# Row stores of tiles 20 to 27 moved from the last attention group to behind the last group's logits

## Chip, cores and metric

The kernel runs on one core of one Trainium2 chip. The metric is the device time of one execution in microseconds (us); the median of several runs is compared.

## The reference

Block-local attention is followed by a mixture of experts that sends each token to one expert. Cut to what matters:

```python
def _attn_ref(q, k, v):              # 8 batches, 8 heads, 576 tokens, 64 dims, chunks of 64
    scores = scale * np.matmul(q_c, k_c.transpose(0, 1, 2, 4, 3))
    attn = softmax(scores)           # over the 64 keys of a chunk
    return np.matmul(attn, v_c)

def _moe_ref(x, w_gate, w1, w2):     # x: 4608 x 512, 8 experts, hidden 1024
    logits = x @ w_gate
    expert_idx = np.argmax(logits, axis=1)
    gate_w = softmax(logits)[arange, expert_idx]
    for e in range(E):
        xe = x[expert_idx == e]
        out[expert_idx == e] = gate_w * (np.maximum(xe @ w1[e], 0) @ w2[e])
```

## The kernel before

**Two phases.** The attention makes 36 tiles of 128 token rows, two tiles (one group) at a time, in the loop `for g in range(NG)` (L1033, 18 groups) and in the straight code behind it (L1098 to L1155), which finishes groups 16 and 17. The experts' phase takes the rows back in expert order, one slot of 256 rows (and up to 128 more) after another. Slot 0 (expert 0) runs already in the gaps of the last groups: `filler(n)` issues n halves of its matmul blocks (L622 and L720 to L722). Slot 1 begins after `make_xt(1, ...)`, L1171 to L1173.

**A group's way.** scores (L238), softmax, transpose (L274), attention times V (`attn_v`, L286), the sums on ScalarE (`soft_d`, L264 and L265), reciprocal (L266) and products (`x_out`, L298 and L301) on VectorE, which write the tile into a row buffer `xb`. Then `x_t` (L310) transposes the tile, `logits` (L322, copied at L1007) computes the gate, `sel_` (L991) and `sums` (L998) collect it.

**Routing.** The tiles are gathered into batches of 6, 6, 6, 6, 4, 4, 2 and 2. When a batch's last logits are summed, the generator `route` is started; `small_op(n)` issues n of its VectorE steps, `advance` its ScalarE and TensorE steps. It ends with `di`, the row of each token in the expert-sorted scratch `xd` in DRAM (L402); `di` has three buffers, so batch 6 writes the one that batch 3 used, and batch 7 that of batch 4. Then GpSimd copies the gate weight and row number into the tile (L404) and the batch's tiles are appended to the list `waiting`.

**Row stores.** `store(n)` (L419) issues an indirect DMA from GpSimd for each of the first n tiles in `waiting` (L426): 128 rows of 528 floats to their places in `xd`. In the loop there is one call at the top of each group (L1038): 2 tiles, in the last group 4. Before it GpSimd makes a one-element copy (`relay`, L1037) that waits for an earlier group's logits copy. Behind the loop there is a call `store(NMAX)` (NMAX is 6) after each of the logits of group 16 (L1114) and 17 (L1127), one at L1139 and one in each turn of the while loop (L1151). Counting through the generators, `waiting` holds tiles 20 to 23 at the top of the last group, 24 to 27 at L1114, 28 to 31 at L1127, 32 and 33 at L1139, and 34 and 35 in the while loop.

**What comes behind the stores.** Every engine works through its instructions in the order in which they are issued here. `gather(1)` (L1153, DMA at L547) brings the rows of slot 1 from `xd`. It may read any row, so it waits until all 36 stores have landed. After it come `gather_x(1)` and the weight loads `load_w(2, 0)` and `load_w(2, 1)` (L529), and on TensorE the transposes of the gathered rows (L570, L605). VectorE computes `early(1)` and `tables` (L482 to L932) as side work once batch 7 is routed; slot 1 needs their results.

Of the kernel before, what the change touches and what calls it, by code (L numbers as in the profile page):

```python
# [25 lines left out]
NG = NTILE // G  # L26
# [4 lines left out]
NMAX = max(BATCHES)  # L31
# [15 lines left out]
def attn_moe_kernel(ctx: ExitStack, tc: tile.TileContext, q, k, v, wg, w, out):  # L47
# [151 lines left out]
    def load_qk(g):  # L199
        if g:  # L200
            qt[g] = ep.tile([P, G, 512], F32, name="qt", bufs=NK)

        if g >= NK:
            nc.sync.dma_start(kb[g % NK], k[g])
            nc.sync.dma_start(qt[g], q[g])
            return
        for i in range(G):
            nc.sync.dma_start(kb[g % NK][:, i, :], k[g, :, i, :])
            if g:
                nc.sync.dma_start(qt[g][:, i, :], q[g, :, i, :])  # L210

    def load_v(g):
        for m in range(2):
            nc.sync.dma_start(vb[g % NB][m::2, m, :, :], v[g, m::2, :, :])
# [10 lines left out]
    def keep(n):  # L225

        for _ in range(n):
            nc.tensor.matmul(pR.rearrange("p (a b) -> p a b", b=P), ones,
                             ones.unsqueeze(1).broadcast_to([P, 4, P]), start=True, stop=True)

    def scores(g):
        ps = pair
        if g == 3:
            nc.tensor.addr_align(64, offset=48, max_nops=0)
        for i in range(G):
            for hp in range(4):
                for po, m, fo, pi, fi, at_ in quads(i, hp):
                    nc.tensor.matmul(ps[po, m, fo], qt[g][pi, i, fi], kb[g % NK][pi, i, fi],  # L238
                                     start=True, stop=True, tile_position=at_)
        return ps  # L240
# [7 lines left out]
    def soft_a(ps):  # L248
        mx = sm.tile([P, NH, 1], F32, name="mx", bufs=2)
        ex = sp.tile([P, NH // 2, 64, 2], F32, name="ex", bufs=2)  # L250
        p4 = ps.rearrange("p m (h k) -> p m h k", k=64)
        m4 = mx.rearrange("p (m h) o -> p m h o", m=2)
        nc.vector.tensor_reduce(m4.rearrange("p m h o -> p m (h o)"), p4, AX.X, ALU.max)
        nc.vector.tensor_tensor(ex.rearrange("p h k m -> p m h k"), p4, m4.broadcast_to(p4.shape), ALU.subtract)
        return ex

    def soft_b(ex):
        nc.scalar.activation(ex, ex, AF.Exp, scale=0.125)
# [10 lines left out]
    def attn_t(ex, banks="UV"):  # L269
        at = sp.tile([P, G, 4, 128], F32, name="at", bufs=1)  # L270
        for i in range(G):
            pt = bank(banks[i], [P, 4, 128])
            for hp in range(4):
                nc.tensor.transpose(pt[:, hp, :], ex[:, i * 4 + hp, :, :].rearrange("p k m -> p (k m)"), ident)  # L274
            nc.scalar.copy(at[:, i, :, :], pt)
        return at
# [3 lines left out]
    def attn_v(g, at):  # L280
        for i in range(G):
            for hp in range(4):
                to = one["UV"[i]][:, hp * 130:(hp + 1) * 130] if hp < 3 else px3[:, i * 131:i * 131 + 130]
                for c in range(2):
                    po = slice(c * 64, (c + 1) * 64)
                    nc.tensor.matmul(to[po, :], at[:, i, hp, po], vb[g % NB][:, :, hp * 2 + c, i * 65:i * 65 + 65],  # L286
                                     start=True, stop=True, tile_position=(0, c * 64))
# [17 lines left out]
    def x_t(g, xt):  # L305
        xT = sp.tile([P, 4, G * P], F32, name="xT1", bufs=1)
        for i in range(G):
            pxt = bank("TQ", [P, 4, 128])
            for kc in range(4):
                nc.tensor.transpose(pxt[:, kc, :], xt[:, (g * G + i) % RB, kc * 128:(kc + 1) * 128],  # L310
                                    ident)
            nc.scalar.copy(xT[:, :, i * P:(i + 1) * P], pxt)
        return xT
# [105 lines left out]
    def store(n, after=None):  # L419

        for k, (b, i, t, di) in enumerate(waiting[:n]):
            x = xb[t // RB % XB][:, t % RB, :]
            if k == 0 and after is not None:
                nc.scalar.copy(x[:, XW - 1:XW], after)
            stored.add(t)
            nc.gpsimd.indirect_dma_start(  # L426
                out=xds[t],
                out_offset=bass.IndirectOffsetOnAxis(ap=di[:, i, :], axis=0),
                in_=x, in_offset=None, bounds_check=NT - 1, oob_is_err=False)
        del waiting[:n]  # L430
# [4 lines left out]
    def advance(kind, side=False):  # L435


        for x in active:
            if x[1] == kind and x[2] == side and not (kind == "t" and r_live[0]):
                x[1] = next(x[0], "end")  # L440
                if x[1] == "end":
                    active.remove(x)
                return
# [3 lines left out]
    def small_op(n=1):  # L447

        for _ in range(min(n, pace[0])):
            advance("v")  # L450
            pace[0] -= 1
# [536 lines left out]
    def sel_(g):  # L988
        lp = st_l.pop(g)
        for i in range(G):  # L990
            nc.tensor.transpose(p4[:, 3 * i, :], lp[:, i * P:(i + 1) * P], ident)  # L991

    def sums(g):
        b = [i for i in range(NBAT) if first[i] <= g * G][-1]
        if g * G == first[b]:
            lgs[0] = sm.tile([P, NMAX, E], F32, name="lg", bufs=2)[:, 0:BATCHES[b], :]
        o = g * G - first[b]
        nc.vector.tensor_reduce(lgs[0][:, o:o + G, :],  # L998
                                p4.rearrange("p a (c e) -> p a e c", e=32)[:, 0::3, 0:E, :], AX.X, ALU.add)
        if (g + 1) * G == first[b + 1]:  # L1000
            r = route(b, lgs[0])
            active.append([r, next(r), False])

    def logits(g):
        if g in st_x:
            lp, pp = logits_p(g, st_x.pop(g))
            nc.scalar.copy(lp, pp)  # L1007
            st_l[g] = lp

    def pauses():  # L1010
        for x in list(active):
            if x[1] is None:
                x[1] = next(x[0], "end")
                if x[1] == "end":
                    active.remove(x)
# [17 lines left out]
    for g in range(NG):  # L1033
        ga, gl = g - 1, g - 2
        pace[0] = 1000
        if waiting:
            nc.gpsimd.tensor_copy(relay, st_l[gl - 1][:, 0:1])  # L1037
        store(2 if g + 1 < NG else 4)  # L1038
        ps = scores(g)
        keep((6, 0, 0)[min(g, 2)])  # L1040
        if g + NK < NG:
            load_qk(g + NK)
        if g + 1 < NG:
            load_v(g + 1)
        if g == 0:
            nc.sync.dma_start(wg_sb[:, :, 0:E], wg)
        if g == 2:
            nc.gpsimd.memset(oh_b, 0.0)
            for t in (*xg[0], *xg[1], xg3):
                nc.gpsimd.memset(t, 0.0)  # L1050

        if gl >= 1:
            sel_(gl - 1)
        if ga >= 0:
            at = attn_t(st_e[ga])
            if g + 1 == NG:
                st_e[g] = soft_a(ps)
            st_e.pop(ga)
        if gl >= 0:
            st_x[gl] = x_t(gl, xb[gl * G // RB % XB])  # L1060
        if g + 1 < NG:
            st_e[g] = soft_a(ps)
            soft_b(st_e[g])
        else:
            soft_b(st_e[g])

            c2.close()
            psum = ctx.enter_context(tc.tile_pool(name="psum", bufs=1, space=PSUM))
            slots["S"] = [psum.tile([P, 512], F32, name=f"psS{i}") for i in range(2)]
            turns["S"] = 0  # L1070
        if gl >= 1:
            sums(gl - 1)
        pauses()
        for x in casts:
            next(x, None)
        casts.clear()
        advance("t")
        if g + 1 < NG:
            small_op(5)
        if ga >= 0:  # L1080
            attn_v(ga, at)
            ri = soft_d()
        if g + 1 == NG:

            c3.close()
            xtp = ctx.enter_context(tc.tile_pool(name="xtp", bufs=1, side="right", reuse_waits="tile"))
            hp_ = ctx.enter_context(tc.tile_pool(name="hp", bufs=HB, side="right", reuse_waits="tile"))
            xhi = xtp.tile([P, 4, BLK + EXT], F32R, name="xhi")
            xlo = xtp.tile([P, 4, BLK + EXT], F32R, name="xlo")
        logits(gl)  # L1090
        cast(g)
        if ga >= 0:
            x_out(ga, ri, xb[ga * G // RB % XB])
        small_op(2)
        advance("a")
        side_op(4)

    g = NG - 1  # L1098
# [12 lines left out]
    logits(g - 1)  # L1111
    x_out(g, ri, xb[g * G // RB % XB])
    small_op(5)
    store(NMAX)  # L1114
    filler(2)
    sel_(g - 1)
    sums(g - 1)
# [195 lines left out]
```

## Time and profile before

| what | us |
|---|---|
| median of 3 runs | 574.8 |
| the runs | 572.28, 574.8, 576.16 |
| profiled execution, its own time | 572.48 |
| its span, first to last instruction | 570.2 |
| TensorE busy in the span | 552.2 |
| VectorE busy | 405.9 |
| ScalarE busy | 281.9 |
| GpSimd busy | 239.2 |

Times in the trace count from the start of the span. PE is TensorE, PEld its weight loads, DVE VectorE, ACT ScalarE, POOL GpSimd. In a timeline a row gives start, duration, engine, line, operation, output<-inputs, the count of merged instructions, and in brackets how long the engine had been idle and whose event came last before it went on ("issue": nothing that the profile shows). An indirect DMA's row on POOL is the time to issue it, not that of its transfer.

### The profile page before, as it was taken

How to read it: one execution, taken by the hardware profiler on the slowest of the kernel's cores; microseconds unless marked ns; L12 is line 12 of the kernel's file. 1: busy time of each engine (PE TensorE's matmuls, PEld its weight loads, DVE VectorE, ACT ScalarE, POOL GpSimd, SP SyncE). 2: the span in 40 equal slices, each digit the busy share in tenths (PEclk: the TensorE clock that was granted, in tenths of full speed). 3: DMA queues.
4: the chain of work that ended last, by engine and by line, in shares of the span. 5: the costliest groups of instructions: out<-in, count | busy, mean ns of one | idle time of the engine just before them, and what ended most of it. 6: DMA issues, size and time to landing. Idle time of an engine off the chain costs nothing.

```text
span 570.2 us, 13170 instructions
## 1 busy us (share of the span) xinstructions
PE 552.2 (97%) x4699; PEld 488.0 (86%) x4699; DVE 405.9 (71%) x907; ACT 281.9 (49%) x519; POOL 239.2 (42%) x271
## 2 busy tenths in 40 slices
PE   7999999869999999999999999999999999999995
PEld 5888888758798899899998999898999988898994
DVE  6788889634776987888867875676757566766663
ACT  5587877522134644646544654354434344444332
POOL 3036753745424553354440843162425235251422
PEclk9999999979999999999999999999999999999998
DMA  8999999333575632236534543465622346211201
GB/s 308 395 366 368 410 408 396 112 123 125 197 252 185 219 99 61 76 115 207 164 94 165 208 123 123 131 236 182 225 58 81 115 152 217 63 42 29 67 1 58
DMA packets 46564, 99.17 MB, mean 174 GB/s; under 512 B 13184, under 2 KB 26496, under 8 KB 42880
## 3 DMA queue, kind: packets, MB, share of 16 engines
q0 software_dynamic: 18352, 58.30, 29.2%
q1 hardware_dynamic: 27824, 38.98, 19.5%
q8 instruction: 67, 1.10, 0.8%
q10 hardware_dynamic: 288, 0.52, 0.2%
q14 instruction: 33, 0.27, 0.1%
HBM read 106.73 MB, written 20.22 MB: 223 GB/s over the span
## 4 chain that ended last, share of the span: by engine, by line
PE 85%; issue 6%; DVE 3%; DMA 2%; POOL 1%; ACT 1%; another core or an unknown queue 0%; POOLq 0%; DVEq 0%; SPq 0%; ACTq 0%
PE psS L622 24%; PE psL L622 8%; PE psU L722 4%; PE psU L720 4%; PE psU L721 4%; PE psV L720 4%; PE psV L721 4%; PE psV L722 4%; PE psS L238 3%; PE psU L286 2%; PE psV L286 2%; PE psL L322 2%; PE psK L735 2%; PE psK L733 2%; PE psS L626 2%
## 5 line engine op out<-in xcount | busy, mean ns | idle before, releaser
L77 DVE TENSOR_TENSOR wlo<-raw,whi 128x1024 fp32r<-128x1024 f32 x110 | 134.3, 1221 | 17.0 <-ACT whi L76 12.2
L671 ACT ACTIVATE h<-psS 128x384 fp32r<-128x384 f32 x84 | 41.3, 492 | 172.5 <-issue 127.6
L529 POOL DMA_INDIRECT raw<-in_w,widx x58 | 66.4, 1145 | 121.3 <-DVE wlo L77 54.1
L622 PE MATMUL psS<-xhi,whi 128*128 128x256 f32 (+2 forms) x368 | 114.4, 313 | 1.4 <-issue 0.7
L76 ACT CAST whi<-raw 128x1024 fp32r<-128x1024 f32 x110 | 114.8, 1043 | 0.3 <-issue 0.3
L622 PE MATMUL psS<-xhi,wlo 128*128 128x256 f32 (+2 forms) x368 | 113.6, 311 | 0.7 <-issue 0.7
L622 PE MATMUL psS<-xlo,whi 128*128 128x256 f32 (+2 forms) x312 | 96.8, 310 | 0.4 <-issue 0.4
L748 POOL DMA_INDIRECT out_y<-y,oid x40 | 42.4, 1060 | 107.0 <-ACTq L653 34.5
L630 DVE SCALAR_TENSOR_TENSOR hl<-psS,h 128x256 fp32r<-128x256 f32 x84 | 35.6, 424 | 59.1 <-ACT h L671 57.2
L547 POOL DMA_INDIRECT xg<-xd,idx x49 | 63.4, 1295 | 30.7 <-issue 16.7
L622 PEld LDWEIGHTS psS<-xhi,whi 128*128 128x128 f32 x368 | 69.9, 190 | 5.4 <-DVE h L630 0.8
L622 PEld LDWEIGHTS psS<-xhi,wlo 128*128 128x128 f32 x368 | 69.7, 189 | 1.5 <-issue 0.9
L622 PEld LDWEIGHTS psS<-xlo,whi 128*128 128x128 f32 x312 | 59.1, 189 | 3.6 <-issue 1.2
L720 PE MATMUL psU<-whi,h 128*128 128x512 f32 x120 | 48.4, 403 | 0.0
L720 PE MATMUL psV<-whi,h 128*128 128x512 f32 x120 | 47.3, 395 | 0.0
L721 PE MATMUL psU<-wlo,h 128*128 128x512 f32 x120 | 47.3, 394 | 0.0
L721 PE MATMUL psV<-wlo,h 128*128 128x512 f32 x120 | 47.1, 393 | 0.0
L722 PE MATMUL psU<-whi,hl 128*128 128x512 f32 x112 | 44.1, 393 | 0.0
L722 PE MATMUL psV<-whi,hl 128*128 128x512 f32 x112 | 44.0, 393 | 0.0
L426 POOL DMA_INDIRECT xd<-xb,di x32 | 31.6, 987 | 16.1 <-issue 12.9
L622 PE MATMUL psL<-xhi,whi 128*128 128x320 f32 (+2 forms) x112 | 34.9, 312 | 0.0
L622 PE MATMUL psL<-xlo,whi 128*128 128x320 f32 (+2 forms) x112 | 34.9, 312 | 0.0
(253 smaller groups left out, 1111.6 us busy)
## 6 DMA issues: line engine op xcount, KB each, us to landing
vb<-in_v SPq DMA_DIRECT2D x36, 260.0 KB
kb<-in_k SPq DMA_DIRECT2D x16, 512.0 KB
qt<-in_q SPq DMA_DIRECT2D x16, 512.0 KB
xg<-xg SPq DMA_DIRECT2D x208, 32.0 KB
raw<-in_w SPq DMA_DIRECT2D x16, 256.0 KB
kb<-in_k SPq DMA_DIRECT2D x4, 256.0 KB
raw<-in_w,widx POOLq DMA_INDIRECT x58
xg<-xd,idx POOLq DMA_INDIRECT x49
```

The costliest lines, as they stand in the source:

```text
L76: nc.scalar.copy(hi, src)
L77: nc.vector.tensor_tensor(lo, src, hi.bitcast(F32), ALU.subtract)
L426: nc.gpsimd.indirect_dma_start(out=xds[t], out_offset=bass.IndirectOffsetOnAxis(ap=di[:, i, :], axis=0), in_=x, in_offset=None, bounds_che ...
L529: nc.gpsimd.indirect_dma_start(out=raw[c][:, :], out_offset=None, in_=w, in_offset=bass.IndirectOffsetOnAxis(ap=widx[:, u, c:c + 1], axis= ...
L547: nc.gpsimd.indirect_dma_start(out=t[:, :], out_offset=None, in_=xd[0:rows, :], in_offset=bass.IndirectOffsetOnAxis(ap=place(u, h), axis=0 ...
L622: nc.tensor.matmul(ph, a, b[:, kc, WIDE - ph.shape[1]:WIDE], start=kc + i == 0, stop=kc + i == 5 and not late)
L630: nc.vector.scalar_tensor_tensor(o, ph, 0.0, hi.bitcast(F32), ALU.max, ALU.subtract)
L671: nc.scalar.activation(hx[:, EXT:EXT + WIDE], ph, AF.Relu)
L720: nc.tensor.matmul(py, hh, wh, start=f == 0, stop=False)
L721: nc.tensor.matmul(py, hh, wl, start=False, stop=False)
L722: nc.tensor.matmul(py, hl, wh, start=False, stop=f == 7)
L748: nc.gpsimd.indirect_dma_start(out=outs[m], out_offset=bass.IndirectOffsetOnAxis(ap=oid[u % 3][:, m:m + 1], axis=0), in_=y, in_offset=None ...
```

## The change

The call at the top of the last group stores nothing (the tiles stay in `waiting`), and the call after group 16's logits is gone. Tiles 20 to 27 thus stay in the list until the call at L1127, which takes six tiles at a time.

```diff
         if waiting:
             nc.gpsimd.tensor_copy(relay, st_l[gl - 1][:, 0:1])
-        store(2 if g + 1 < NG else 4)
+        store(2 if g + 1 < NG else 0)
         ps = scores(g)
@@
     logits(g - 1)
     x_out(g, ri, xb[g * G // RB % XB])
     small_op(5)
-    store(NMAX)
     filler(2)
     sel_(g - 1)
```

By the list's order the calls now take: L1127 tiles 20 to 25, L1139 tiles 26 to 31, the first turn of the while loop 32 and 33, a later turn 34 and 35. The number of stores, their sizes and their order are as before.

## Rows read from the trace of the kernel before

**Rows 1.** The page: the span, and the chain that ended last, by engine

```profile
span 570.2 us, 13170 instructions
PE 85%; issue 6%; DVE 3%; DMA 2%; POOL 1%; ACT 1%; another core or an unknown queue 0%; POOLq 0%; DVEq 0%; SPq 0%; ACTq 0%
```

**Rows 2.** Busy time by stretch, of the last group and what follows it

```profile
core 0: us, PE busy (x) PEld busy (x) DVE busy (x) ACT busy (x) POOL busy (x), PEclk, DMA share, GB/s
115.00:122.00 7.00, 4.15 (x30) 2.31 (x26) 0.08 (x2) 0.18 (x1) 5.21 (x9) 0.97 0.55 211
122.00:128.00 6.00, 4.13 (x18) 3.74 (x19) 4.06 (x19) 2.31 (x9) 0.31 (x2) 0.50 0.06 23
132.00:140.00 8.00, 7.60 (x52) 6.22 (x50) 2.80 (x19) 1.05 (x8) 5.40 (x9) 1.00 0.54 206
140.00:150.00 10.00, 10.00 (x62) 8.95 (x63) 8.93 (x51) 1.49 (x4) 5.36 (x6) 1.00 0.34 107
```

**Rows 3.** Timeline of POOL: stores, the copy for batch 5, first gather of slot 1

```profile
110.83 1.02 POOL L426 DMA_INDIRECT xd<-xb,di  x1 [0.16 <-issue]
...
118.84 0.98 POOL L426 DMA_INDIRECT xd<-xb,di  x1 [0.30 <-issue]
120.12 0.97 POOL L426 DMA_INDIRECT xd<-xb,di  x1 [0.30 <-issue]
...
127.46 0.31 POOL L404 COPY xb<-ft 128x4 f32<-128x4 f32 x2 [6.17 <-DVE ft L393]
131.03 0.99 POOL L426 DMA_INDIRECT xd<-xb,di  x1 [3.26 <-issue]
...
137.73 0.97 POOL L426 DMA_INDIRECT xd<-xb,di  x1 [0.30 <-issue]
...
141.96 0.97 POOL L426 DMA_INDIRECT xd<-xb,di  x1 [0.30 <-issue]
145.68 1.03 POOL L547 DMA_INDIRECT xg<-xd,idx  x1 [2.75 <-DVE ns L869]
```

**Rows 4.** Timeline of all engines beside the first eight stores

```profile
112.77 0.89 PE L286 MATMUL psU<-vb,at 128*64 128x130 f32 x12
...
115.10 0.39 PE L286 MATMUL psT<-vb,at 128*64 128x130 f32 x4
...
118.09 0.18 ACT L264 ACTIVATE su<-psU 128x6 f32<-128x6 f32 x1 [3.49 <-PE psL L322]
...
119.48 0.38 PE L622 MATMUL psS<-xhi,wlo 128*128 128x256 f32 x1 [0.69 <-issue]
...
122.46 0.17 ACT L265 ACTIVATE su<-psT 128x2 f32<-128x2 f32 x1 [4.19 <-PE psS L622]
...
122.80 0.25 DVE L266 RECIPROCAL ri<-su 128x16 f32<-128x16 f32 x1 [7.72 <-ACT su L265]
```

**Rows 5.** Timeline of an earlier group, with a pair of stores

```profile
86.73 0.98 POOL L426 DMA_INDIRECT xd<-xb,di  x1 [0.31 <-issue]
...
88.82 0.39 PE L286 MATMUL psT<-vb,at 128*64 128x130 f32 x4
...
89.67 0.16 ACT L264 ACTIVATE su<-psU 128x6 f32<-128x6 f32 x1
...
90.04 0.25 DVE L266 RECIPROCAL ri<-su 128x16 f32<-128x16 f32 x1
```

**Rows 6.** Timeline from group 17's logits to slot 1's transposes

```profile
128.75 0.64 PE L322 MATMUL psL<-xT,wg_sb 128*32 128x256 f32 x8
...
134.17 0.17 DVE L402 TENSOR_REDUCE di<-dst 128x2 int32<-128x16 f32 x1 [0.50 <-DMA xd<-xb,di]
...
139.00 0.39 ACT L633 ACTIVATE h<-psS 128x256 fp32r<-128x256 f32 x1 [5.05 <-PE psS L622]
...
139.76 0.16 DVE L402 TENSOR_REDUCE di<-dst 128x2 int32<-128x16 f32 x1
...
149.88 0.63 PE L570 MATMUL psQ<-ident,xg 128*128 128x128 f32 x4
...
150.53 0.14 DVE L932 CAST kind<-vb 128x1 int32<-128x1 f32 x1
```

**Rows 7.** Chain in order of time (start, duration, what): a store's landing

```profile
131.03 2.59 DMA xd<-xb,di
```

## The prediction

> **What bounds the kernel now.** I read the page first: the chain that ended last is TensorE for 85% of a span of 570.2 us [rows 1]. So a change pays by the time at which TensorE gets on with the experts' slots, and the place where this change can move that is the stretch from the last group to slot 1's transposes, about 110 to 156 us. From slot 1 on nothing is edited, and I carry any gain or loss at slot 1's start to the end one for one.
>
> The table by stretch shows what is wrong there [rows 2]. From 115 to 122 us TensorE is busy only 4.15 of 7 us, VectorE 0.08 and ScalarE 0.18, while GpSimd is busy 5.21. Right behind it, from 122 to 128 us, TensorE's granted clock is 0.50. From 132 us on TensorE is full again (7.60 of 8, 10.00 of 10): it has slot 0's fillers.
>
> The timeline of that hole [rows 4]: TensorE's products for psU start at 112.77 and for psT end at 115.10 + 0.39 = 115.49, yet ScalarE reads psU only at 118.09 and psT at 122.46, and VectorE's reciprocal, idle for 7.72 us, comes at 122.80. TensorE itself stops 0.69 us for "issue" before matmuls whose operands are long there. In an earlier group the same ScalarE read comes at 89.67, 0.46 us behind the end of psT (88.82 + 0.39 = 89.21), and the reciprocal at 90.04, 0.83 behind it; a pair of stores had just been issued there too, the second at 86.73 [rows 5]. What is particular to the last group is a train of eight stores, the first at 110.83 and the last at 120.12, with two more just ahead of it [rows 3]. A second train (six stores, 131.03 to 137.73, with a shorter wait at 5.05 us on ScalarE until 139.00 [rows 3, 6]) also makes results come late, but TensorE runs on. So I take the trains as the cause: results of TensorE come late while more than a pair of stores is under way. The trace shows this as a coincidence in time, twice; it shows no mechanism.
>
> **What the change removes.** The train at 110.83 goes. If it is the cause, the reciprocal comes 0.83 us behind psT as in the earlier group, at 115.49 + 0.83 = 116.3 instead of 122.80: 6.5 us earlier. TensorE then doesn't go hungry, and the stretch at half clock goes too: 4.13 us of busy time at 0.50 [rows 2] would be about 2.1 us at full. Logits of group 17, now at 128.75 [rows 6], would start at 128.75 - 6.5 - 2.1 = 120.2. That is the gain on offer: 8.6 us for TensorE, 6.5 us for GpSimd and VectorE.
>
> **What it moves.** The eight stores are not gone: all 16 stores of tiles 20 to 35 now start behind the copy for batch 5 (L404), which in GpSimd's order precedes the call at L1127. That copy waits for VectorE; it is at 127.46 now, so at 127.46 - 6.5 = 121.0 then. With two copies (0.31) and 0.3 between instructions [rows 3] the first store goes at 121.6. Stores follow each other every 120.12 - 118.84 = 1.28 us [rows 3]. From the first to the last are 15 steps, 19.2 us; in between stand four or five small copies of GpSimd for batches 6 and 7, about 0.2 us each like those of 127.46, 0.9 together. The last store starts at 121.6 + 19.2 + 0.9 = 141.7. Now it starts at 141.96 [rows 3]. So **the queue on GpSimd gives back nearly all of the gain**: 0.3 us is left.
>
> Behind the last store the gather of slot 1 waits for the landing, 2.59 us after a store's start [rows 7], and for the semaphores of all of them: 145.68 - 141.96 = 3.7 us [rows 3]. The gather would start at 141.7 + 3.7 = 145.4. TensorE's transposes come 149.88 - 145.68 = 4.2 us behind it [rows 3, 6]. If the landing is what they wait for, that distance stays, and they start at 149.6, 0.3 us earlier. If the landing is earlier than that (a store's 2.59 is the nearest row, so about 148.3 now and 148.0 then), up to 1.9 us can be gained. I take 0.3: the 4.2 is the row of this very gather.
>
> **The waits that are new.** `di` of batch 6 and 7 overwrites the buffer of batch 3 and 4, so VectorE waits at L402 until stores 18 to 23, and 24 to 27, have landed. That wait is visible already (0.50 us on a store's DMA at 134.17 [rows 6]). Now the store of tile 23 starts at 121.6 + 3 x 1.28 = 125.4 and lands at 128.0; VectorE would be there at about 134.17 - 8.6 = 125.6, so it waits 2.4 us. Tile 27 starts at 121.6 + 7 x 1.28 + 0.5 = 131.1 and lands at 133.7; VectorE would be there at 139.76 - 8.6 = 131.2 and waits 2.5 us more. Behind VectorE stand the low halves of h, for which slot 0's second matmuls wait. The cover is the gap that opened: TensorE's fillers need 149.88 - 128.75 = 21.1 us [rows 6] from the logits on, so they would be through at 120.2 + 21.1 = 141.3, and the gathered rows are not there before 149.6. That leaves 8.3 us in which stalls cost nothing. VectorE's tables, 150.53 - 139.76 = 10.8 us behind the last `di` [rows 6], end at 133.7 + 10.8 = 144.5 instead of 150.53 and cease to matter. Without the cover the two waits would cost 4.9 us.
>
> **The sum.** 0.3 us off the profiled execution's 572.48: 572.2 us. That execution lies 2.3 us below the median of the runs, 574.8. On the median's scale I expect 574.5.
>
> **Rivals.**
>
> *The clock falls again.* If TensorE runs out of fillers at about 141 to 145 and stands until the gathered rows come, it does what it did at 115 to 122, and the next matmuls run at half clock. Price by rows 2: 2.1 us of lost time, if as much work falls into it as at 122 to 128; the whole six-microsecond stretch filled would lose 3.0. With the 0.3 gained that is 574.3 to 575.2 on the profile's scale, 576.6 to 577.5 on the median's. For it: the 8.3 us of empty time. Against it: late results will stretch the fillers into that time. The Trainium skill, page "TensorE: Matmul & The Clock Gate", section "HAM oscillation — how this bites in real kernels", says that a TensorE which waits for a DMA between pieces of work is throttled and begins the next piece cold. By that rule this rival would hold; the trace agrees in the one case it has (0.50 behind the hole).
>
> *The long train stalls TensorE twice as much (slower).* Sixteen stores instead of eight. If lateness grows with their number, the hole of 6.5 us becomes 13.0, plus 2.1 of half clock: fillers end at 141.3 + 15.1 = 156.4 instead of 149.88, 6.5 us later: 579.0, on the median's scale 581.3. It decides once the stalls exceed the 8.3 us of cover. For it: TensorE's 0.69 us stops in the first train [rows 4]. Against it: in the second train of six TensorE was busy 7.60 of 8 us [rows 2].
>
> *The stores are not the cause.* Then the hole stays, the copy for batch 5 stays at 127.46, the last store starts at 128.1 + 20.1 = 148.2, 6.2 us later than now, and with it the gather: 578.7, or 581.0. Against it: both late stretches coincide with trains and none lies outside.
>
> *The gain goes through.* If the stores left GpSimd faster than every 1.28 us, TensorE's 8.6 us would remain: 563.9, or 566.2. Rows 3 speak against it: within trains the pitch is the issue itself, 0.97 busy and 0.30 between.
>
> **How the numbers follow.** Within 1% of the median is 569.1 to 580.5; that is about what a measurement of this kernel can tell from no change. Forecast (-2 to +1 us) 0.52; clock 0.24; long train 0.12, of which two thirds end beyond 1%; stores not the cause 0.06, half of it beyond 1%; gain through 0.06. Faster 0.06, slower 0.11, same 0.83. The range runs from the gain of 1.9 us and the runs' own scatter of 2.5 below the median, 574.5 - 1.6 - 2.5 = 570.4, to just short of the long train's 581.3, 580.6.
>
> **What would show it.** Right: in the changed kernel VectorE's reciprocal (L266) at about 116 and not 122.8, no stretch at half clock at 122 to 128, the first of 16 stores at 121 to 122, pitch 1.28, the last at 141 to 142, the gather at 145 to 146, slot 1's transposes at 149 to 150; waits of VectorE at L402 on store DMAs. Wrong: a reciprocal still at 122; stores later than 142; TensorE idle after 141 followed by half clock; fillers (L622) with 0.69 us "issue" stops through 123 to 141 and done only after 150.

## The result, and the profile after

The kernel after takes 576.32 us (median of 20 runs, 575.19 to 578.91), the kernel before 573.21 us beside it (20 runs, 571.29 to 576.16): a ratio of 1.0057, with a 95% interval of 1.0043 to 1.0071. That is 3.1 us slower (2.5 to 4.1), where the forecast was 0.3 us faster. The profiled execution of after has a span of 573.9 us against 570.2 [rows 1], 3.7 us more.

The record gives no number for the chip of this measurement; it is called A here. The experiments below ran on four numbered chips, B to E; kernels sent together shared a chip and the kernel before beside them, and their times are compared with that alone. That A is none of these four is inferred from the times: no run of the kernel before lies under 571.29 us here or over 563.04 us there.

The table by stretch of after, on chip A (busy time of each engine, then the granted clock of TensorE):

```profile
core 0: us, PE busy (x) PEld busy (x) DVE busy (x) ACT busy (x) POOL busy (x), PEclk, DMA share, GB/s
115.00:122.00 7.00, 6.93 (x78) 5.73 (x78) 5.14 (x25) 3.61 (x14) 0.31 (x2) 1.00 0.00 0
122.00:128.00 6.00, 5.97 (x46) 5.24 (x46) 2.99 (x16) 1.18 (x7) 4.49 (x5) 1.00 0.42 158
128.00:132.00 4.00, 3.88 (x23) 3.11 (x21) 0.69 (x5) 0.00 (x0) 3.23 (x6) 1.00 0.56 207
132.00:140.00 8.00, 2.56 (x12) 1.89 (x13) 1.63 (x11) 0.53 (x3) 6.17 (x7) 0.81 0.57 221
140.00:150.00 10.00, 8.28 (x22) 5.45 (x23) 4.04 (x22) 1.04 (x3) 5.24 (x7) 0.50 0.42 136
```

Read against [rows 2], the hole has moved. The stretch 115 to 122 is full now (6.93 of 7 against 4.15), and 122 to 128 runs at full clock (1.00 against 0.50). But 132 to 140, full before (7.60 of 8), is busy only 2.56, and 140 to 150 runs at a granted clock of 0.50 against 1.00, the lower of its two levels (1.2 and 2.4 GHz).

The timeline of after, all engines, answering [rows 3, 4, 6]:

```profile
116.78 0.25 DVE L266 RECIPROCAL ri<-su 128x16 f32<-128x16 f32 x1 [0.80 <-ACT su L265]
121.03 0.64 PE L322 MATMUL psL<-xT,wg_sb 128*32 128x256 f32 x8
121.56 0.31 POOL L404 COPY xb<-ft 128x4 f32<-128x4 f32 x2 [7.69 <-DVE ft L393]
122.29 1.01 POOL L426 DMA_INDIRECT xd<-xb,di  x1 [0.42 <-issue]
...
127.40 0.28 PE L622 MATMUL psS<-xhi,wlo 128*128 128x256 f32 x1
...
130.99 0.17 DVE L402 TENSOR_REDUCE di<-dst 128x2 int32<-128x16 f32 x1 [4.92 <-issue]
133.69 0.38 ACT L633 ACTIVATE h<-psS 128x256 fp32r<-128x256 f32 x1 [7.34 <-remote]
134.59 0.39 PE L622 MATMUL psS<-xhi,whi 128*128 128x256 f32 x1 [2.70 <-issue]
...
141.83 0.97 POOL L426 DMA_INDIRECT xd<-xb,di  x1 [0.31 <-issue]
142.10 0.58 PE L721 MATMUL psU<-wlo,h 128*128 128x512 f32 x1 [1.30 <-issue]
145.09 0.66 ACT L633 ACTIVATE h<-psS 128x256 fp32r<-128x256 f32 x2 [10.87 <-remote]
145.51 0.42 DVE L630 SCALAR_TENSOR_TENSOR h<-psS,h 128x256 fp32r<-128x256 f32 x1 [9.51 <-ACT h L633]
145.56 1.04 POOL L547 DMA_INDIRECT xg<-xd,idx  x1 [2.75 <-remote]
...
155.23 0.63 PE L570 MATMUL psQ<-ident,xg 128*128 128x128 f32 x4
...
159.83 0.85 PE L626 MATMUL psS<-xlo,whi 128*128 128x320 f32 x4
```

The reader sees here: the reciprocal at 116.78 instead of 122.80, group 17's logits at 121.03 instead of 128.75, the first of 16 stores at 122.29 and the last at 141.83, and the gather of slot 1 at 145.56 instead of 145.68. Then ScalarE, which takes slot 0's matmul results at L633, stands 7.34 and 10.87 us ("remote" is an event whose sender the profile doesn't have), VectorE behind it 9.51 us, and TensorE stops again and again for "issue". The result that ScalarE reads at 133.69 was finished at 127.40 + 0.28 = 127.68, 6.0 us earlier (0.04 us for the same result in the kernel after on chip C, 124.95 behind 124.91). The fillers that needed 149.88 - 128.75 = 21.1 us [rows 6] need 155.23 - 121.03 = 34.2 us. Slot 1's transposes start at 155.23, right behind the fillers, as they did before (neither row has an idle time in brackets): they are 5.35 us later than before, though the gather is not later at all. The second matmuls of slot 1 (L626) come at 159.83, in the trace of before at 155.72, so 4.1 us of it are left there:

```profile
155.72 0.85 PE L626 MATMUL psS<-xlo,whi 128*128 128x320 f32 x4
```

### The profile page after: what moved, and what is told of

Read it like the earlier page. It is cut to its first block, busy times and chain, and to the rows that moved or that the text cites. A ratio compares the mean times of both kernels' runs of the same rounds, so it can differ in the third digit from the quotient of the medians.

```text
span 573.9 us, 13166 instructions
## 1 busy us (share of the span) xinstructions
PE 553.9 (97%) x4699; PEld 488.3 (85%) x4699; DVE 407.1 (71%) x907; ACT 281.4 (49%) x519; POOL 239.8 (42%) x271
## 4 chain that ended last, share of the span: by engine, by line
PE 86%; issue 4%; another core or an unknown queue 3%; DVE 3%; ACT 1%; POOL 1%; DMA 0%; POOLq 0%; DVEq 0%; ACTq 0%
PE psS L622 25%; PE psL L622 8%; PE psU L720 4%; PE psU L722 4%; PE psU L721 4%; PE psV L720 4%; PE psV L721 4%; PE psV L722 4%; PE psS L238 3%; PE psU L286 2%; PE psV L286 2%; PE psL L322 2%; PE psK L735 2%; PE psK L733 2%
## 5 line engine op out<-in xcount | busy, mean ns | idle before, releaser
L630 DVE SCALAR_TENSOR_TENSOR hl<-psS,h 128x256 fp32r<-128x256 f32 x84 | 35.5, 423 | 58.9 <-ACT h L671 55.2
L630 DVE SCALAR_TENSOR_TENSOR h<-psS,h 128x128 f32 (+1 forms) x92 | 27.1, 295 | 11.8 <-ACT h L633 9.5
```

The costliest lines, as they stand in the source:

```text
L630: nc.vector.scalar_tensor_tensor(o, ph, 0.0, hi.bitcast(F32), ALU.max, ALU.subtract)
```

## The experiments

The theories at the start. *Train*: while a long train of row stores is under way, TensorE's reports come late; 16 stores in one train make a longer hole than eight. *Buffer*: the new waits at L402 for the three `di` buffers hold VectorE and with it the fillers. *Queue*: what costs is the place of the stores in GpSimd's queue ahead of slot 1's gather.

**Five `di` buffers instead of three, on the kernel after (chip B).** It takes the new waits away by taking away what makes them.

```diff
-        di = small("di", I32, 1, 3)
+        di = small("di", I32, 1, 5)
```

> The changed kernel with five buffers for di instead of three, so that VectorE need not wait at L402 for the landing of stores 18 to 27. Theory 'train' (while a long train of row stores is under way, TensorE's finished work is reported late, and TensorE itself stops): the loss stays, +2.5 to +3.5 us against before; the 4.9 us wait at L402 is gone, but ScalarE's waits of 7.3 and 10.9 us before L633 are still there within 2 us. Theory 'buffer' (the new wait at L402 holds VectorE, and with it slot 0's fillers): the loss goes, -1 to +1 us against before, and ScalarE's waits before L633 fall under 4 us.

Measured: 570.19 us against 561.68 before, a ratio of 1.0155 (1.014 to 1.0169). Timeline of this kernel:

```profile
124.58 0.17 DVE L402 TENSOR_REDUCE di<-dst 128x2 int32<-128x16 f32 x1
126.96 0.16 DVE L402 TENSOR_REDUCE di<-dst 128x2 int32<-128x16 f32 x1
...
144.29 1.03 POOL L547 DMA_INDIRECT xg<-xd,idx  x1 [2.75 <-DMA xd<-xb,di]
...
147.80 1.13 PE L570 MATMUL psQ<-ident,xg 128*128 128x128 f32 x4 [7.56 <-DMA xg<-xd,idx]
```

No `di` waits, and a loss of 8.5 us (the kernel after itself was not run on this chip; on chip C it lost 7.9): the buffer theory falls for the loss seen here. But there is no hole either. ScalarE's waits ahead of L633 are 2.44 us at most, the kernel before itself takes 11.5 us less than on chip A, and TensorE stands 7.56 us for the DMA of the gathered rows. What the train theory expected of ScalarE was not seen on this chip, and what five buffers would do on chip A was not tested.

**The two edits apart, each on the kernel before (chip B).** First the call at the top of the last group alone; the other call then takes its four tiles and two more.

```diff
-        store(2 if g + 1 < NG else 4)
+        store(2 if g + 1 < NG else 0)
```

> Only the first half of the change: nothing is stored at the top of the last group, the call after group 16's logits stays and takes tiles 20 to 25. Theory 'train': the first train is six stores from about 113 us instead of eight from 111, so a hole in TensorE's reports comes back at 115 to 122 us, VectorE's reciprocal at 119 to 122 instead of 116.8; then 26 to 31 and four more as before's second train. Time -1 to +2 us against before. Theory 'buffer': stores 18 to 27 land early enough, no loss: -1 to +1.

Measured: 561.9 us, ratio 1.0007 (0.9996 to 1.0018): no difference. Second the call behind group 16's logits alone:

```diff
     small_op(5)
-    store(NMAX)
     filler(2)
```

> Only the second half of the change: four stores at the top of the last group stay, the call after group 16's logits is gone, tiles 24 to 35 follow behind group 17's logits as a train of twelve. Theory 'train': four stores hold the reciprocal to about 118 us (2 to 4 us less than before's 122.8), and the train of twelve costs ScalarE one wait of 7 to 10 us before L633: -2 to +2 us against before. Theory 'buffer': stores 18 to 23 are early, only 24 to 27 are late: about +1 us.

Measured: 564.56 us, ratio 1.0049 (1.0037 to 1.0061). First the one, by stretch and in the timeline, then the other:

```profile
115.00:122.00 7.00, 7.00 (x63) 6.16 (x62) 5.19 (x29) 3.19 (x11) 5.37 (x9) 1.00 0.50 194
122.00:128.00 6.00, 5.86 (x44) 5.10 (x43) 3.42 (x22) 1.06 (x7) 4.78 (x5) 1.00 0.60 223
```

```profile
112.67 1.01 POOL L426 DMA_INDIRECT xd<-xb,di  x1 [0.16 <-issue]
113.88 0.25 DVE L266 RECIPROCAL ri<-su 128x16 f32<-128x16 f32 x1 [0.80 <-ACT su L265]
...
136.37 1.04 POOL L547 DMA_INDIRECT xg<-xd,idx  x1 [2.75 <-DVE vb L910]
139.98 0.75 PE L570 MATMUL psQ<-ident,xg 128*128 128x128 f32 x4 [1.00 <-DMA xg<-xd,idx]
```

```profile
138.30 1.03 POOL L547 DMA_INDIRECT xg<-xd,idx  x1 [2.75 <-DVE yn L921]
141.74 0.75 PE L570 MATMUL psQ<-ident,xg 128*128 128x128 f32 x4 [2.28 <-DMA xg<-xd,idx]
```

In the first kernel 16 stores follow one another from 112.67 to 132.60 with hardly a pause. The reciprocal (113.88) comes too early in this train to be a test of it, but TensorE stays busy 7.00 of 7 and 5.86 of 6 us beside it, at full clock. So a long train alone does not make the hole. The price follows the gather: at 136.37 nothing, at 138.30 2.9 us.

**Eight indirect reads in the old place, on the kernel after (chip B).** GpSimd issues eight indirect reads of 128 rows of 512 weights each into a weight buffer, four where each of the two calls stood, so it is as busy there as with the eight stores, but nothing is stored.

```diff
...
+            nc.gpsimd.indirect_dma_start(
+                out=raw[j // 4][:, j % 4 * 512:(j % 4 + 1) * 512], out_offset=None,
+                in_=w.rearrange("r (a b) -> (r a) b", b=512), in_offset=bass.IndirectOffsetOnAxis(ap=some, axis=0),
+                bounds_check=16 * E * P - 1, oob_is_err=False)
...
+        if g + 1 == NG:
+            reads(range(4))
...
+    reads(range(4, 8))
```

> The changed kernel plus eight indirect reads of 2 KB rows (128 rows each, from the weights into SBUF that is free then) issued by GpSimd where the kernel before had its eight early stores. If what matters is a train of indirect DMAs on GpSimd, whatever its direction: VectorE's reciprocal of group 17 comes at 120 us or later instead of 116.8, with TensorE's 0.69 us issue stops at L622 around 117 to 121. If only writes to DRAM matter: reciprocal at 116 to 118, no hole there.

Measured: 573.1 us (one run) against 561.68, 11.4 us more. The reciprocal is in time (115.89), the waits of VectorE at L402 are 5.35 and 2.46 us, and the gather starts at 146.42. The reads make no hole, but on this chip stores make none either, so this doesn't tell reads from stores. They lengthen GpSimd's queue: the gather is 3.4 us later than in the kernel after on chip C (143.00, below).

**Both kernels again, unchanged (chip C).**

> The kernel before, unchanged, to have its trace on the chip that this set of runs gets. In the four runs above, trains of 12 to 16 row stores left TensorE's reports on time, and the kernel before took 561.7 us there, 11.5 less than in its first 20 runs. Theory 'hole depends on the chip': where the kernel before takes about 562 us, the reciprocal of group 17 comes at 114 to 117 us and slot 1's transposes at 138 to 142; where it takes about 573 us, the reciprocal comes at 120 us or later. Theory 'train' in its plain form (any train makes the hole): reciprocal at about 122 on every chip.

> The changed kernel, unchanged, on the same chip as the kernel before. Where there is no hole, all 16 stores queue on GpSimd from about 121 us, the gather of slot 1 goes at about 144.5 and TensorE waits for it: +7 to +9 us against before. Where there is a hole: +2.5 to +4 us, as first measured.

Measured: after 569.73 us (5 runs) against 561.81 (9 runs), ratio 1.0144 (1.0124 to 1.0163), 7.9 us. First the kernel before, by stretch and in the timeline:

```profile
115.00:122.00 7.00, 7.00 (x66) 6.31 (x66) 5.30 (x25) 3.25 (x11) 5.76 (x12) 1.00 0.54 206
122.00:128.00 6.00, 6.00 (x46) 5.25 (x45) 3.72 (x26) 1.09 (x7) 4.81 (x7) 1.00 0.57 215
```

```profile
110.96 1.02 POOL L426 DMA_INDIRECT xd<-xb,di  x1 [0.17 <-issue]
...
114.60 0.25 DVE L266 RECIPROCAL ri<-su 128x16 f32<-128x16 f32 x1 [0.80 <-ACT su L265]
131.25 0.97 POOL L426 DMA_INDIRECT xd<-xb,di  x1 [0.30 <-issue]
134.96 1.04 POOL L547 DMA_INDIRECT xg<-xd,idx  x1 [2.74 <-DVE vb L881]
...
139.24 0.63 PE L570 MATMUL psQ<-ident,xg 128*128 128x128 f32 x4
...
144.09 0.75 PE L626 MATMUL psS<-xlo,whi 128*128 128x320 f32 x4
```

The same train of eight stores from 110.96 on, and TensorE busy 7.00 of 7 and 6.00 of 6 at full clock, the reciprocal at 114.60 instead of 122.80 [rows 4], the gather at 134.96 instead of 145.68 [rows 3]. The kernel after on the same chip:

```profile
140.00:150.00 10.00, 4.23 (x18) 3.24 (x17) 3.65 (x19) 0.78 (x2) 5.82 (x7) 0.75 0.44 123
```

```profile
119.69 1.01 POOL L426 DMA_INDIRECT xd<-xb,di  x1 [0.42 <-issue]
...
127.66 0.17 DVE L402 TENSOR_REDUCE di<-dst 128x2 int32<-128x16 f32 x1 [4.36 <-DMA xd<-xb,di]
131.71 0.17 DVE L402 TENSOR_REDUCE di<-dst 128x2 int32<-128x16 f32 x1 [2.90 <-DMA xd<-xb,di]
...
139.24 1.01 POOL L426 DMA_INDIRECT xd<-xb,di  x1 [0.31 <-issue]
143.00 1.04 POOL L547 DMA_INDIRECT xg<-xd,idx  x1 [2.75 <-DVE kind L932]
146.51 1.13 PE L570 MATMUL psQ<-ident,xg 128*128 128x128 f32 x4 [5.77 <-DMA xg<-xd,idx]
...
152.90 0.75 PE L626 MATMUL psS<-xlo,whi 128*128 128x320 f32 x4
```

With no hole to remove, the change costs what GpSimd's queue loses by it. Its train of 16 begins at 119.69 instead of 110.96, 8.73 us later, because GpSimd now stands idle (7.7 us) until the copy for batch 5; the last store is 7.99 us later, the gather 143.00 - 134.96 = 8.04. TensorE stands 5.77 us for the rows, and its first matmuls then take 1.13 us instead of 0.63, at half clock (granted clock 0.50 from 146.50 to 150.00). The Trainium skill, page "TensorE: Matmul & The Clock Gate", section "HAM oscillation — how this bites in real kernels", says that a wait for a DMA leaves TensorE throttled for the work behind it; the trace agrees here (0.75 as the mean granted clock of 140 to 150 us).

**Row stores as plain DMAs from SyncE, on the kernel after (chips C and D).**

```diff
-            nc.gpsimd.indirect_dma_start(
-                out=xds[t],
-                out_offset=bass.IndirectOffsetOnAxis(ap=di[:, i, :], axis=0),
-                in_=x, in_offset=None, bounds_check=NT - 1, oob_is_err=False)
+            nc.sync.dma_start(xds[t][t * P:(t + 1) * P, :], x)
```

> The changed kernel with every row store as a plain DMA from SyncE: tile t goes to rows 128t to 128t+127 of the scratch instead of its expert's places (so tokens meet the wrong experts; amounts of work and bytes stay). GpSimd issues no store. If GpSimd's issue at 1.28 us each is what delays slot 1's gather: the last store leaves before 135 us, and the gather starts 8 us or more before the changed kernel's; time 6 us or more below the changed kernel. If a train of writes to DRAM makes the hole: ScalarE's waits of 7 us and more before L633 are there also with SyncE's stores; if it is GpSimd's way of issuing them, they are not.

> The kernel after, with the row stores as plain DMAs from SyncE, tile t to rows 128t of the scratch, so that tokens meet the wrong experts (the same amount of work). Where the hole is there: if GpSimd's indirect stores make it, no hole and about 560 us; if the bytes moved or the chip make it, the hole stays and the time is near 573. Where it is not there: 559.6 us, as seen before, since GpSimd's queue is free.

Measured: 559.62 us on chip C (before 561.81) and 560.3 on chip D (before 560.23), one run each. The stores stand as late as in the kernel after, but not in GpSimd's queue: the gather starts at 130.68 and 131.04, and nothing is lost. Nothing is gained clearly either, for TensorE is full in the kernel before on these chips. The loss belongs to GpSimd's queue, not to the later place in the program. (Plain stores don't read `di` either, so the new waits at L402 go with them; the five buffers showed that these aren't the loss.)

**Half rows, on the kernel after (chip C) and on the kernel before (chip D).**

```diff
-    xd = dpool.tile([NT, XW], F32, name="xd")
+    xd = dpool.tile([NT, XW // 2], F32, name="xd")
@@
-                in_=x, in_offset=None, bounds_check=NT - 1, oob_is_err=False)
+                in_=x[:, XW // 2:XW], in_offset=None, bounds_check=NT - 1, oob_is_err=False)
@@
-            out=t[:, :], out_offset=None, in_=xd[0:rows, :],
+            out=t[:, XW // 2:XW], out_offset=None, in_=xd[0:rows, :],
```

> The changed kernel with the scratch and each row store and gather cut to the second half of a row (1056 of 2112 bytes; the first half of x is left out). If GpSimd's issue sets the pace, the stores still follow each other every 1.28 us and the gather starts within 0.5 us of the changed kernel's. If the bytes in flight make the hole (where there is one), it shrinks to half or less; if the number of stores does, it stays.

> The kernel before, with only the second half of each row stored and gathered (the first half of x doesn't reach the experts): the same number of stores, half the bytes. Where the hole is there: if the number of descriptors makes it, the reciprocal stays at about 122.8; if the bytes make it, it comes well before that, 116 to 119. Where it is not there: near the kernel before, within 1 us, since GpSimd's pitch of 1.28 us was the same for half rows.

Measured: 568.15 us against 561.81, and 558.73 against 560.23, one run each. Two neighbouring stores and the gather of the half-row kernel after:

```profile
122.62 0.97 POOL L426 DMA_INDIRECT xd<-xb,di  x1 [0.30 <-issue]
123.89 0.97 POOL L426 DMA_INDIRECT xd<-xb,di  x1 [0.30 <-issue]
...
143.00 1.04 POOL L547 DMA_INDIRECT xg<-xd,idx  x1 [2.43 <-DVE kind L932]
145.85 1.13 PE L570 MATMUL psQ<-ident,xg 128*128 128x128 f32 x4 [5.08 <-DMA xg<-xd,idx]
```

Half the bytes leave the pitch at 1.28 us (1.27 between these two) and the gather where it was. What a store takes of GpSimd was the same with 528 and with 264 floats to a row. The Trainium skill, page "Perfetto Trace Analysis", section "DMA Instruction — SWDGE (GPSIMD)", says that the profiled end of such a DMA is the end of generating descriptors, not of the transfer; the trace agrees, 0.97 us with whole rows and with half rows. On the kernel before, half rows gave 1.5 us in one run; the expectation was within 1 us, and one run does not tell the two apart.

**Pauses between pairs of stores, on the kernel before (chips D and E).** Three fills on GpSimd behind each second store of tiles 20 to 35 (chip D), or of tiles 20 to 27 alone (chip E, the condition `20 <= t < 28`). They were made for a chip with the hole, to see whether it stays when no more than two stores follow each other; no run met such a chip.

```diff
+            if t >= 20 and t % 2:
+                for _ in range(3):
+                    nc.gpsimd.memset(rest_, 0.0)
@@
+    rest_ = const.tile([P, 512], F32, name="rest_")
```

> The kernel before, with three fills of a 128x512 tile on GpSimd behind every second store from tile 20 on, so that no more than a pair of stores follows without a pause. Theory of the trains (where the hole is there): reciprocal at about 116 instead of 122.8, no half clock behind it. Theory of GpSimd's queue (everywhere): eight pauses of about 1.6 us, some 12 us, stand ahead of slot 1's gather, of which those behind tile 28 count; where no hole hides it, the gather comes 6 to 13 us later than in the kernel before and the time rises by 5 to 11 us (567 to 573). If the queue were not what costs, the time would stay near 562.

> The kernel before, with three fills of a 128x512 tile on GpSimd (about 1.65 us) behind each second store of tiles 20 to 27 alone: four pauses in the early train. Theory of GpSimd's queue: where no hole is, the gather comes 4 x 1.65 = 6.6 us later, less what the queue was idle ahead of it, about 5 to 6.6; with 0.8 us of cover the time rises by 4 to 6 us over the kernel before on the same chip. Theory of the trains, where the hole is (before near 573): no more than a pair of stores without a pause, so the reciprocal comes at about 116 instead of 122.80, and the time is below the kernel before. If spacing is not what counts there, the reciprocal stays at 122 and the time rises.

> The kernel before, unchanged, for a look at its train of eight stores on whichever chip this is. Two levels have been seen: 573.2 us with a hole at 115 to 122 us (reciprocal L266 at 122.80), and 561.7 to 561.8 us without one (reciprocal at 114.60). If the hole belongs to the chip, the time is near one of the two levels, and the reciprocal says which; if it comes and goes with the execution, a time between them, or both forms in the timed runs beside it, may be seen.

Measured on chip D: 574.13 us against 560.23 and 561.48 (the kernel before, twice; its reciprocal at 115.27, so no hole), above the 567 to 573 expected: the pauses hardly found idle time in the queue, and the gather came 12.1 us later. On chip E: 568.4 against 561.41, 7.0 us, a little above the 4 to 6 expected. The wait of TensorE, first on chip D, then on chip E:

```profile
151.16 1.12 PE L575 MATMUL psQ<-ident,xg 128*128 128x128 f32 x4 [10.16 <-DMA xg<-xd,idx]
```

```profile
145.75 1.13 PE L575 MATMUL psQ<-ident,xg 128*128 128x128 f32 x4 [5.17 <-DMA xg<-xd,idx]
```

**All together.** The start of slot 1's gather, from the profile of each kernel, and the time over the kernel before of the same chip:

| kernel | chip | gather at | over before, us |
|---|---|---|---|
| after, plain stores from SyncE | C, D | 130.68, 131.04 | -2.2, +0.1 |
| before, half rows | D | 133.86 | -1.5 |
| before | C, D | 134.96, 135.63 | 0 |
| top call only | B | 136.37 | +0.2 |
| second call only | B | 138.30 | +2.9 |
| before, four pauses | E | 142.42 | +7.0 |
| after | C | 143.00 | +7.9 |
| after, half rows | C | 143.00 | +6.3 |
| after, five `di` buffers | B | 144.29 | +8.5 |
| after, eight reads | B | 146.42 | +11.4 |
| before, eight pauses | D | 147.70 | +13.9 |

The plain stores, half rows, reads and pauses were timed once each. Up to about 136.4 the gather costs next to nothing. From there the loss follows it nearly one for one across the chips. In the traces, against "top call only" (gather at 136.37, L626 at 145.53), L626 comes 1.90 us later for a gather 1.93 us later in "second call only", whose granted clock stays at 1.00 behind its wait of 2.28 us. In the five kernels with whole rows and a gather behind 140 it comes 0.5 to 1.1 us later than the gather's delay alone would make it (five buffers: 8.44 for 7.92; eight pauses: 12.45 for 11.33); behind their waits of 5.17 to 10.16 us the granted clock was 0.50, and the excess is put down to that. Whether the queue is lengthened by moving stores, by reads or by idle fills makes little difference.

## Why the prediction was wrong

**What bounds the kernel; carrying a change at slot 1 to the end.** Held: 4.1 us at L626 on chip A stand against 3.7 in the span and 3.1 in the medians, and on chip C 152.90 - 144.09 = 8.8 us at L626 against 8.7 in the span.

**What the change removes.** Held on chip A, nearly to the number: reciprocal at 116.78 (116.3 foretold), logits at 121.03 (120.2), no half clock at 122 to 128. The train of eight was the hole's companion there. But that the train by itself is the cause falls: on chips C and D the same train leaves VectorE idle for 0.80 us ahead of the reciprocal and not 7.72, and on chip B a train of 16 leaves TensorE all but full (7.00 of 7 and 5.86 of 6 us).

**What it moves.** Held: first store 122.29 (121.6), pitch 1.28, last 141.83 (141.7), gather 145.56 (145.4). GpSimd's queue gave the whole gain back.

**From the gather to the transposes, 4.2 us.** Misread and too long: in [rows 6] the transposes follow the fillers without idle time, so the 4.2 us were no wait for rows. Where TensorE waited for whole rows, they came 3.3 to 3.6 us behind the gather's start (3.51 on chip C). On chip A it didn't matter.

**The new waits at L402.** There as foretold: 4.92 us with the label "issue" on chip A, and 4.36 and 2.90 us on store DMAs on chip C, against 2.4 and 2.5 foretold. They were mis-sized. Where there is no hole they are not the loss: with five buffers it is as large. On chip A the trace speaks against them too: the one wait there ended at 130.99, and TensorE stood on until 134.59, right behind VectorE's L630 and ScalarE's L633 (133.69), which reads the result finished at 127.68. No run tested it on chip A.

**The cover of 8.3 us: the step that failed.** The fillers were to be through at 141.3, with stalls that fit into the time up to 149.6. They were through at 155.23: the stalls and the half clock came to 34.2 - 21.1 = 13.1 us. By the table by stretch TensorE stood idle 0.12 + 5.44 + 1.72 = 7.3 us between 128 and 150, and its 8.28 us of work at half clock from 140 to 150 lost 4.1 more; the other 1.7 us are not broken down. Of the 13.1 us, the 7.7 us by which the logits came earlier paid for a part; 5.35 us were left at slot 1's transposes. That the time still came out near the forecast is luck: the lead of 7.7 us, which was to be cover only, happened to pay for most of 13.1 us that the sum did not have. This is the rival "the long train stalls TensorE twice as much", with its 15.1 us of stalls and half clock, which I gave 0.12. The evidence that I set against it was the second train of before, in which TensorE was busy 7.60 of 8 us [rows 2]. That row was the wrong neighbour: six stores (131.03 to 137.73 [rows 3]) against sixteen in one train in after. The longer train of before, the eight stores beside the hole at 115 to 122 [rows 2, 3], was nearer, and that hole I took to vanish with the move rather than to move with it. Why TensorE's reports come late beside the stores stays open, as said below.

**The rival "the stores are not the cause"** has the mechanism of chips B to E, though not its own story: there the hole doesn't stay, it isn't there. Its arithmetic, a longer queue ahead of the gather and TensorE waiting for it, was priced at 6.2 us; measured were 7.9. What was set against it, that no late stretch lies outside the trains, was an oversight. In the trace of before, no row store starts between 92.45 and 106.75, yet from 100 to 105 us TensorE is busy 4.19 of 5 us (5.00 on chip C) and stops for "issue" beside two gathers (the first at 100.27):

```profile
101.62 1.01 POOL L547 DMA_INDIRECT xg<-xd,idx  x1 [0.30 <-PE psL L322]
102.39 0.25 PE L238 MATMUL psS<-kb,qt 64*64 64x64 f32 x1 [0.33 <-issue]
103.12 0.83 PE L238 MATMUL psS<-kb,qt 64*64 64x64 f32 x38 [0.48 <-issue]
```

The kernel after on chip A has the same stops there (0.48 and 0.39 us). So on that chip the lateness is not a matter of row stores alone.

**"The clock falls again"** was right in its rule and came as a companion of the larger losses, not alone: half clock from 140 to 150 us on chip A, and on the others behind the waits for the gather of 5.08 to 10.16 us; behind those of 1.00 and 2.28 us the granted clock stayed at 1.00.

**What stays open** is what makes TensorE's reports late on chip A. By the times it was there in every run of the kernel before (571.29 us the lowest of 20, against medians and single runs of 560.23 to 561.81 on the others), and on none of four other chips with the same kernel. Whether it goes with the chip or with something else that differed between the first measurement and the experiments is not separated. It isn't the train's length alone, as the 16 stores on chip B show, nor indirect DMAs from GpSimd alone: from 160 us on, GpSimd goes on issuing them on chip A, and TensorE has no further stop for "issue". That a chip with the hole would lose it with spaced pairs of stores, with half the bytes, or with SyncE issuing them, was not seen, because no run came to such a chip. So the cause of the loss on chip A is read from one trace of each kernel, not shown by an experiment; the cost of GpSimd's queue, on the other chips, is shown by the kernels of the table.

No kernel here clearly beats the kernel before: with the call at the top moved alone it is the same, and with GpSimd freed of the stores altogether the same too.

## What to carry to other kernels

A stall that sits beside a burst of DMAs may go along when the burst is moved: before its disappearance is counted as a gain, ask what work will stand where the burst then is, and price the stall there once more with the longer burst. In GpSimd's queue the gather stands behind the stores, here 1.28 us each with whole rows and with half rows, so a train that begins later holds up the gather by nearly as much (8.73 us and 8.04 on chip C); what that costs is the delay less the slack between the fillers' end and the rows' landing, and 0.5 to 1.1 us more where half clock followed the wait. And what one trace shows as a coincidence in time may belong to where and when it was taken.

## What the runs showed of the hardware that I had not expected

- The same kernel takes 573.2 us in one measurement and 560.2 to 561.8 on four chips in the others; at the stretch of the hole the granted clock was 1.00 and TensorE full on chips C and D.
- An indirect store of 128 rows keeps GpSimd 0.97 us and the next follows 1.28 us behind it, with 528 floats in a row and with 264.
- DMA traffic alone doesn't hold TensorE's results up: on chip C the kernel before is full in the stretch with a DMA share of 0.57.
